# Attention with a sliding window and routed experts: the attention steps put in the order of the array's tiling

## The chip, the cores and the metric

One core of one Trainium2 chip runs the program. The metric is the device time of one execution in microseconds (us). A core has five engines that run their own instruction lists and wait for each other by semaphores: TensorE (PE, with the loads of its stationary operand shown apart as PEld), VectorE (DVE), ScalarE (ACT), GpSimd (POOL) and SyncE (SP, which only issues DMAs here). Each engine works through its list in order.

## The reference

Eight batches of eight heads: 512 local positions and 32 global ones, head size 64. A local query sees the 32 global keys and the local keys within 32 positions; a global query sees all 544 keys. Then every token goes through one of eight experts, chosen by a gate and sticky along the sequence.

```python
s_g = scale * q_g @ k_all.T;  out_g = softmax(s_g) @ v_all
s_ll = where(abs(pos_i - pos_j) <= 32, scale * q_l @ k_l.T, -1e9)
a_l = softmax(concat([scale * q_l @ k_g.T, s_ll]))
out_l = a_l @ concat([v_g, v_l])
x = concat([out_g, out_l])              # per batch: 544 tokens, 512 wide
e = argmax(x @ w_gate)  or the expert before it, by a local gate
out = p[e] * (relu(x @ w1[e]) @ w2[e])
```

## The kernel before

The first third of the program is attention, the rest the experts; the change is in attention alone. The work of a batch is six units: four local ones, `l0` to `l3`, each a pair of heads, and two global ones, `g0` and `g1`, each two pairs. They follow each other as l0 l1 g0 l2 g1 l3, batch after batch, 48 in all, and the loop in `run` makes one step for each of them. In the step of unit number s, the scores and exponentials of unit s are made, and the probabilities of unit s-2 are transposed and multiplied with v. So in the step that is called l1 below, the scores are those of l1 and the v products are those of l3 of the batch before.

What a step is made of, by its functions:

- `l_s` makes one half (`hb` 0 or 1) of a local unit's scores: a matmul writes the mask into a PSUM bank (bf16, all 128 columns of the array), then eight products of 128 rows by 64 columns add q k. `g_s` makes the scores of a global unit, also 64 columns wide.
- `l_max` on DVE takes the row maxima of such a bank and subtracts them; `l_exp` on ACT takes the exponential. The second half's exponential is put off into the step after (`late`). `g_max` and `g_exp` do this for a global unit.
- `l_t` and `g_t` transpose the probabilities on PE (128 by 128) into two banks, and ACT copies each bank to SBUF.
- `l_av` multiplies one half with v: sixteen products, 32 columns wide, into one bank. DVE then adds 1e-9 to the row sums (`rs`), takes their reciprocal and writes the scaled result to `xa`: three instructions, the last of which reads the bank for the last time. `g_av` is the same for a global unit, with `xg`.
- Pieces of the gate's logits are put in between: `f1` transposes 128 columns of a batch's `xa` on PE (four transposes, then a copy by ACT), `f1g` transposes `xg`, `f2` and `f2g` multiply with the gate's weights (32 columns wide), and `f3` transposes the logits back. They wait in the list `fin` and are taken from it in order; a piece can't be taken in the step that put it there. After the v products of a local unit its `f1` is put into the list.

PSUM has eight banks. Scores take four in turn (`ps_s`), transposes two (`ps_t`: `l_t`, `g_t`, `f1`, `f1g`), and the products with v two (`ps_o`: `l_av`, `g_av`, `f2`, `f2g`, and one small product of `f3`). A bank is written again when its last reader is done.

The order of each engine's list is that of the calls in `run`. PE matmuls have three tilings here: 128, 64 and 32 columns of the array. In a local step before, PE's order is: transposes, mask, scores of half 0, perhaps a piece, v product of half 0, mask, scores of half 1, perhaps a piece, v product of half 1.

Of the kernel before, what the change touches and what calls it, by code (L numbers as in the profile page):

```python
# [13 lines left out]
ALU = mybir.AluOpType  # L14
AX = mybir.AxisListType
# [3 lines left out]
P = 128  # L19
# [80 lines left out]
class Attn:  # L100
# [122 lines left out]
    def bank(self, r):  # L223
        return r().rearrange("p (t k) -> p t k", k=P)

    def l_s(self, st, hb):
        nc = self.nc
        if hb == 0:
            b, pr = st["u"]
            if pr == 0:  # L230
                self.cur[b]["xa"] = self.xa()
                self.cur[b]["xg"] = self.xg()
            st["pe"] = self.pe()
        qbd = st["qbd"]
        kf = st["kx"].rearrange("p m c k -> p (m c k)")
        sp = st["sp"] = self.bank(self.ps_s)
        mo = sp.rearrange("p t (k c) -> p t k c", c=32)[:, :, 0::3, :]
        nc.tensor.matmul(mo, self.cst.idb, self.mask[:, 4 * hb:4 * hb + 4], start=True, stop=False, skip_group_check=True)
        for t in range(4):
            for t2 in range(2):  # L240
                w = 8 * hb + 2 * t + t2
                f = 32 * (3 * (w // 2) + w % 2)
                nc.tensor.matmul(sp[64 * t2:64 * t2 + 64, t], qbd[:, w], kf[:, f:f + P], start=False, stop=True, skip_group_check=True)  # L243

    def l_max(self, st, hb):
        nc = self.nc
        mx = self.mx()
        nc.vector.tensor_reduce(out=mx, in_=st["sp"], axis=AX.X, op=ALU.max)  # L248
        self.drip()
        nc.vector.tensor_tensor(out=st["pe"][:, 4 * hb:4 * hb + 4], in0=st["sp"], in1=mx.broadcast_to([P, 4, P]), op=ALU.subtract)  # L250

    def l_exp(self, st, hb):
        pe = st["pe"][:, 4 * hb:4 * hb + 4]
# [166 lines left out]
    def run(self, rt, moe):  # L420
        order = []
        for b in range(B):
            order += [("l", b, 0), ("l", b, 1), ("g", b, 0), ("l", b, 2), ("g", b, 1), ("l", b, 3)]
        units = [{"k": k, "u": (b, i)} for k, b, i in order]
        pairs = [u for u in units if u["k"] == "l"]
        n = len(units)
        fin = []
        when = []

        def fpiece():  # L430
            if fin and when[0] <= s:
                f, a = fin.pop(0)
                when.pop(0)
                if f is not None:
                    f(*a)
# [12 lines left out]
        self.prep(pairs[0])  # L448
        self.blank(1)
        nc.vector.memset(self.pg.t[1], 0.0)  # L450
        npr, late = 0, None
        for s in range(n):
            nx = units[s]
            st = units[s - 2] if s >= 2 else None
            nl = nx["k"] == "l"
            sl = st is not None and st["k"] == "l"
            sg = st is not None and not sl
            if nl:
                if npr + 2 < len(pairs):
# [12 lines left out]
            if sg:  # L472
                self.g_t(st)
            if late is not None:
                self.l_exp(late, 1)
                late = None
            if nl:
                self.l_s(nx, 0)
                self.l_max(nx, 0)
            else:  # L480
                self.g_s(nx)
                self.g_max(nx)
            fpiece()
            if sl:
                self.l_av(st, 0)
            if nl:
                self.l_exp(nx, 0)
                self.l_s(nx, 1)
                self.l_max(nx, 1)
            fpiece()  # L490
            if not nl:
                self.g_exp(nx)
            if sl:
                self.l_av(st, 1)
            if sg:
                self.g_av(st)
            if nl:
                if s in DEFER:
                    late = nx
                else:  # L500
                    self.l_exp(nx, 1)
            if s == 0:
                self.cst.load()
                self.cst.rest()
                self.gens += [self.setup(), rt.setup()]
            if s < 6:
                self.drip(4)
# [12 lines left out]
        self.drip(1000)  # L520
        moe.tail = self.tail(units[n - 2], units[n - 1], fin, rt, moe)

    def tail(self, sg, sl, fin, rt, moe):
        b = B - 1
        fin = [x for x in fin if x[0] is not None]
# [36 lines left out]
        yield from every(rt.kinds(), 3)  # L562
        yield KINDS
        yield from every(rt.rest(self.ps_o), RE)
# [1004 lines left out]
```

## Time and profile before

| What | Value |
|---|---|
| median of 3 runs (lowest, highest) | 706.22 us (705.49, 707.1) |
| the profiled execution | 705.68 us |
| its span, first to last instruction | 704.0 us |
| mean granted clock of TensorE | 0.985 |
| PE, DVE, ACT, POOL busy in the span | 673.2, 428.2, 343.3, 197.7 us |

The profile is of one execution; its span is 1.7 us shorter than its time, and its time 0.5 us below the median. Attention's steps fill the first 230 us or so; the first matmul of the experts starts at 233.75 us. A batch in the middle of attention can be followed by the transposes of `g0` (line 328, in step g1), which start at 102.58 us in one batch and at 130.36 us in the next: 27.78 us for six steps.

### The profile page before, as it was taken

To read this page: it belongs to the slowest core of one execution; us is meant where nothing else is said; L and a number is where in the kernel's file an instruction comes from. 1 tells how busy PE (TensorE), PEld (TensorE's weight loads), DVE (VectorE), ACT (ScalarE), POOL (GpSimd) and SP (SyncE) were. 2 spreads that over 40 slices of the span, in tenths; PEclk is the share of its full clock that TensorE was granted. 3 is DMA by queue.
4 is the path that set the end of the run, shared out by engine and by line. 5 is a ranking of instruction groups with operands and counts; after the bars stand their busy time and mean duration, and the time that the engine had idled before them with its cause. 6 is when DMAs were issued, how large, how long until landed. Compare 5 with 4: busy or idle time off the path is not lost.

```text
span 704.0 us, 18381 instructions
## 1 busy us (share of the span) xinstructions
PE 673.2 (96%) x7253; PEld 564.2 (80%) x7253; DVE 428.2 (61%) x1057; ACT 343.3 (49%) x614; POOL 197.7 (28%) x321
## 2 busy tenths in 40 slices
PE   9999999999899899998998999999999999999991
PEld 7777777777677778887887988889988889899890
DVE  7878777777887787994516625335445325165551
ACT  4565555655355664652325635243535334256551
POOL 7634344243333311132022312040304020223312
PEclk9999999999999999999999999999999999999996
DMA  8966967865756487767319737255557245176561
GB/s 329 383 232 228 354 242 271 324 258 205 292 182 244 173 319 248 269 220 273 131 66 314 241 116 254 70 182 175 195 173 234 98 126 167 65 262 237 187 215 51
DMA packets 43011, 151.44 MB, mean 215 GB/s; under 512 B 7965, under 2 KB 9245, under 8 KB 38688
## 3 DMA queue, kind: packets, MB, share of 16 engines
q1 hardware_dynamic: 35536, 126.92, 50.5%
q0 software_dynamic: 6960, 21.90, 9.3%
q8 instruction: 77, 1.26, 0.7%
q14 instruction: 150, 1.23, 0.6%
q10 hardware_dynamic: 288, 0.13, 0.1%
HBM read 130.55 MB, written 19.69 MB: 213 GB/s over the span
## 4 chain that ended last, share of the span: by engine, by line
PE 59%; DVE 3%; issue 1%; ACT 0%; POOL 0%; DVEq 0%; POOLq 0%; ACTq 0%
PE ps L1262 28%; PE ps L1251 26%; PE ps L1205 3%; DVE wq L1160 1%; DVE wp L1160 0%; PE ps L1374 0%; DVE xT L991 0%; PE ps L999 0%; DVE xl L1160 0%; POOL xa L1191 0%; DVE xT L989 0%; DVE wp L1208 0%; PE ps L276 0%; DVE wq L1366 0%; DVE hh L1160 0%
## 5 line engine op out<-in xcount | busy, mean ns | idle before, releaser
L1268 POOL DMA_INDIRECT out_dram<-y,tk x39 | 40.7, 1042 | 317.9 <-ACT y L1267 297.8
L1262 PE MATMUL ps<-wp,wq 128*128 128x512 f32 x504 | 128.0, 401 | 0.9 <-ACT wq L1365 0.9
L1262 PEld LDWEIGHTS ps<-wp,wq 128*128 128x128 f32 x504 | 93.5, 190 | 20.6 <-ACT wq L1365 1.1
L1251 PE MATMUL ps<-wp,wp 128*128 128x256 f32 (+5 forms) x672 | 109.4, 323 | 0.0
L1251 PEld LDWEIGHTS ps<-wp,wp 128*128 128x128 f32 x672 | 103.8, 189 | 4.8
L1254 DVE SCALAR_TENSOR_TENSOR wq<-ps,wq 128x256 fp32r<-128x256 f32 (+5 forms) x80 | 41.7, 526 | 73.3 <-ACT wq L1253 70.7
L191 POOL TENSOR_SCALAR_AFFINE_SELECT qbd<-raw 64x512 f32<-64x512 f32 x62 | 44.6, 719 | 120.2 <-PE ps L243 100.8
L1208 DVE TENSOR_TENSOR wp<-ps,wp 128x512 fp32r<-128x512 f32 x40 | 27.5, 691 | 79.8 <-ACT wp L1207 79.8
L1253 ACT ACTIVATE wq<-ps 128x256 fp32r<-128x256 f32 (+5 forms) x80 | 37.2, 468 | 78.6 <-PE ps L1251 68.7
L243 PE MATMUL ps<-kx,qbd 128*64 128x128 f32 x1024 | 71.3, 281 | 1.8 <-issue 1.8
L1267 ACT ACTIVATE y<-ps,pp 128x512 f32<-128x512 f32 x39 | 26.9, 690 | 77.3 <-PE ps L1262 71.0
L243 PEld LDWEIGHTS ps<-kx,qbd 128*64 128x64 f32 x1024 | 55.2, 138 | 11.7 <-issue 7.6
L248 DVE TENSOR_REDUCE mx<-ps 128x4 f32<-128x512 f32 x64 | 43.9, 686 | 28.5 <-PE ps L243 28.3
L1160 DVE TENSOR_TENSOR wp<-raw,wp 128x1024 fp32r<-128x1024 f32 x47 | 57.0, 1217 | 2.9 <-ACT wp L1150 2.8
L1191 POOL DMA_INDIRECT xa<-xs,idx x42 | 52.2, 1242 | 17.1 <-issue 10.0
L254 ACT ACTIVATE pe<-pe 128x512 f32<-128x512 f32 x64 | 40.7, 636 | 32.3 <-DVE pe L250 32.3
L1150 ACT CAST wp<-raw 128x1024 fp32r<-128x1024 f32 x49 | 50.8, 1046 | 1.5 <-DMA raw<-in_w_dram 0.7
L1207 ACT CAST wp<-ps 128x512 fp32r<-128x512 f32 x40 | 23.5, 591 | 55.1 <-PE ps L1205 55.1
L250 DVE TENSOR_TENSOR pe<-ps,mx 128x512 f32<-128x512 f32 x64 | 44.1, 688 | 1.6
L276 PE MATMUL ps<-v,pt 128*32 128x65 f32 x2048 | 43.1, 224 | 1.6 <-ACT pe L254 0.6
L276 PEld LDWEIGHTS ps<-v,pt 128*32 128x32 f32 x2048 | 33.7, 111 | 13.1 <-issue 7.5
L191 POOL TENSOR_SCALAR_AFFINE_SELECT kx<-raw 128x384 f32<-128x384 f32 (+3 forms) x127 | 43.1, 372 | 2.9 <-DMA raw<-in_qk_dram 0.8
(279 smaller groups left out, 1172.4 us busy)
## 6 DMA issues: line engine op xcount, KB each, us to landing
raw<-in_w_dram SPq DMA_DIRECT2D x78, 512.0 KB, 3.8
v<-in_vw_dram SPq DMA_DIRECT2D x32, 1040.0 KB, 9.8
raw<-in_qk_dram SPq DMA_DIRECT2D x32, 528.0 KB, 9.4
xa<-in_w_dram SPq DMA_DIRECT2D x26, 512.0 KB, 4.7
xT<-in_w_dram SPq DMA_DIRECT2D x20, 512.0 KB, 4.2
xs<-xa SPq DMA_DIRECT2D x8, 1056.0 KB
qgb<-in_qg_dram SPq DMA_DIRECT2D x8, 128.0 KB
xa<-xs,idx POOLq DMA_INDIRECT x42
```

What stands on the lines that cost most here:

```text
L191: self.nc.gpsimd.affine_select(out=out, in_=in_, pattern=pat, compare_op=ALU.is_ge, fill=0.0, base=0, channel_multiplier=0)
L243: nc.tensor.matmul(sp[64 * t2:64 * t2 + 64, t], qbd[:, w], kf[:, f:f + P], start=False, stop=True, skip_group_check=True)
L248: nc.vector.tensor_reduce(out=mx, in_=st["sp"], axis=AX.X, op=ALU.max)
L250: nc.vector.tensor_tensor(out=st["pe"][:, 4 * hb:4 * hb + 4], in0=st["sp"], in1=mx.broadcast_to([P, 4, P]), op=ALU.subtract)
L254: self.nc.scalar.activation(out=pe, in_=pe, func=AF.Exp, scale=SCALE)
L276: nc.tensor.matmul(o[32 * w4:32 * w4 + 32, g, h], pt[:, 2 * g + w4 // 2, w4 % 2, h, :], v[:, w, h * (D + 1):(h + 1) * (D + 1)], start=True ...
L1150: nc.scalar.copy(out=hi, in_=raw)
L1160: (nc.gpsimd if pool else nc.vector).tensor_tensor(out=lo, in0=raw, in1=hi.bitcast(F32), op=ALU.subtract)
L1191: self.nc.gpsimd.indirect_dma_start(out=self.xr[j] if k == "early" else self.xr4[:, j], out_offset=None, in_=src, in_offset=bass.IndirectO ...
L1251: nc.tensor.matmul(ph, a[:, dc, fs], b_[:, dc, n0:n1], start=(n == 0), stop=(n == 11))
L1254: nc.vector.scalar_tensor_tensor(out=hl[:, fc, n0:n1], in0=ph, scalar=0.0, in1=hh[:, fc, n0:n1].bitcast(F32), op0=ALU.max, op1=ALU.subtract)
L1262: nc.tensor.matmul(py, a[:, fc, js], b_[:, fs], start=(fc == 0 and k == 0), stop=(fc == 7 and k == 2))
```

## The change

The mask's matmuls for both halves get a function of their own, `l_m`, and a step's calls are put into this order: transposes, both masks, pieces that transpose (`f1`, `f1g`, `f3`, up to two), the late exponential, both halves of the scores with their maxima, the exponential of half 0, both halves of the v products, and at the end one piece that multiplies with the gate's weights (`f2` or `f2g`). Each instruction is still issued as often as before.

```diff
+    def l_m(self, st):
...
+        st["sp"] = [self.bank(self.ps_s) for _ in range(2)]
+        for hb in range(2):
+            mo = st["sp"][hb].rearrange("p t (k c) -> p t k c", c=32)[:, :, 0::3, :]
+            nc.tensor.matmul(mo, self.cst.idb, self.mask[:, 4 * hb:4 * hb + 4], start=True, stop=False, skip_group_check=True)
...
-        def fpiece():
-            if fin and when[0] <= s:
+        def fpieces(kinds, most):
+            while most and fin and when[0] <= s and fin[0][0].__name__ in kinds:
...
             if sg:
                 self.g_t(st)
+            if nl:
+                self.l_m(nx)
+            fpieces(("f1", "f1g", "f3"), 2)
             if late is not None:
                 self.l_exp(late, 1)
                 late = None
             if nl:
                 self.l_s(nx, 0)
+                self.l_s(nx, 1)
                 self.l_max(nx, 0)
+                self.l_max(nx, 1)
+                self.l_exp(nx, 0)
             else:
                 self.g_s(nx)
                 self.g_max(nx)
-            fpiece()
+                self.g_exp(nx)
             if sl:
                 self.l_av(st, 0)
-            if nl:
-                self.l_exp(nx, 0)
-                self.l_s(nx, 1)
-                self.l_max(nx, 1)
-            fpiece()
-            if not nl:
-                self.g_exp(nx)
-            if sl:
                 self.l_av(st, 1)
             if sg:
                 self.g_av(st)
+            fpieces(("f2", "f2g"), 1)
...
-                    fin += [(self.f1g, (b,)), (None, ()), (self.f2g, (b,))]
-            if len(fin) > 4:
-                fpiece()
+                    fin += [(self.f1g, (b,)), (self.f2g, (b,))]
```

In the lists below a row is an instruction with its line, what it writes and reads, and its size; `ps_63` to `ps_66` are the banks of the scores, `ps_67` and `ps_68` those of the transposes, `ps_69` and `ps_70` those of the v products. A line of attention has a number that is higher by four after the change (243 is 247, 276 is 280, 352 is 356); the mask is line 238 before and 236 after.

PE in a step l1, before, from the first mask to the transposes of the step after (line 359 is `f1g`):

```order
L238 MATMUL ps_63<-mask,idb 128x4x2x32
L243 MATMUL ps_63<-kx_147,qbd_145 64x128 x8
L359 MATMUL ps_68<-idf,xg_110 128x128
L276 MATMUL ps_70<-v_133,pt_142 32x65 x16
L238 LDWEIGHTS idb
L238 MATMUL ps_64<-mask,idb 128x4x2x32
L243 MATMUL ps_64<-kx_147,qbd_145 64x128 x8
L276 MATMUL ps_69<-v_133,pt_143 32x65 x16
L260 MATMUL ps_67<-idf,pe_137 128x128 x4
L260 MATMUL ps_68<-idf,pe_137 128x128 x4
```

The same place on PE after the change (line 363 is `f1g`, line 379 is `f2g`, line 356 is `f1`):

```order
L236 MATMUL ps_63<-mask,idb 128x4x2x32
L236 LDWEIGHTS idb
L236 MATMUL ps_64<-mask,idb 128x4x2x32
L363 MATMUL ps_68<-idf,xg_110 128x128
L247 MATMUL ps_63<-kx_147,qbd_145 64x128 x8
L247 MATMUL ps_64<-kx_147,qbd_145 64x128 x8
L280 MATMUL ps_70<-v_133,pt_142 32x65 x16
L280 MATMUL ps_69<-v_133,pt_143 32x65 x16
L379 MATMUL ps_70<-xgT_116,wgg 32x32 x4
L264 MATMUL ps_67<-idf,pe_137 128x128 x4
L264 MATMUL ps_68<-idf,pe_137 128x128 x4
L356 MATMUL ps_67<-idf,xa_108 128x128 x4
```

`f1g` has moved ahead of the scores, and `f2g` follows the v products and writes `ps_70`, the bank that the first of them wrote two rows above it; the `f1` of the next step stands ahead of that step's scores.

PE in a step g0, before, from the last scores of g0 on (line 375 is `f2g`, line 352 is `f1`):

```order
L296 MATMUL ps_66<-raw_77,qgb_153 64x288
L296 MATMUL ps_66<-raw_78,qgb_153 64x288
L375 MATMUL ps_70<-xgT_116,wgg 32x32 x4
L276 MATMUL ps_69<-v_134,pt_140 32x65 x16
L352 MATMUL ps_67<-idf,xa_108 128x128 x4
L276 MATMUL ps_70<-v_134,pt_141 32x65 x16
```

The same place on PE after the change (line 300 makes the scores, line 371 is `f2`):

```order
L300 MATMUL ps_66<-raw_77,qgb_153 64x288
L300 MATMUL ps_66<-raw_78,qgb_153 64x288
L280 MATMUL ps_69<-v_134,pt_140 32x65 x16
L280 MATMUL ps_70<-v_134,pt_141 32x65 x16
L371 MATMUL ps_69<-xT,wgl 32x512 x4
```

`f2`, which stood in the step after (step l2), is now at this step's end and writes the bank of the first v product; `f2g` and `f1` have gone to the places shown above.

DVE in a step l1, before (lines 248 and 250 are `l_max`, lines 279, 281 and 284 are the three instructions of `l_av`; lines 771 and 774 are small work of another function):

```order
L248 TENSOR_REDUCE mx_120<-ps_63 128x4
L771 MEMSET xa_109 128x4x7
L250 TENSOR_TENSOR pe_138<-ps_63,mx_120 128x512
L279 TENSOR_SCALAR rs_122<-ps_70 128x4
L774 COPY gx<-tok 32x1
L281 RECIPROCAL rs_122<-rs_122 128x4
L284 TENSOR_TENSOR xa_108<-ps_70,rs_122 128x2x128
L248 TENSOR_REDUCE mx_118<-ps_64 128x4
L250 TENSOR_TENSOR pe_138<-ps_64,mx_118 128x512
L279 TENSOR_SCALAR rs_123<-ps_69 128x4
L281 RECIPROCAL rs_123<-rs_123 128x4
L284 TENSOR_TENSOR xa_108<-ps_69,rs_123 128x2x128
```

The same place on DVE after the change:

```order
L252 TENSOR_REDUCE mx_120<-ps_63 128x4
L254 TENSOR_TENSOR pe_138<-ps_63,mx_120 128x512
L252 TENSOR_REDUCE mx_118<-ps_64 128x4
L254 TENSOR_TENSOR pe_138<-ps_64,mx_118 128x512
L283 TENSOR_SCALAR rs_122<-ps_70 128x4
L285 RECIPROCAL rs_122<-rs_122 128x4
L288 TENSOR_TENSOR xa_108<-ps_70,rs_122 128x2x128
L283 TENSOR_SCALAR rs_123<-ps_69 128x4
L285 RECIPROCAL rs_123<-rs_123 128x4
L288 TENSOR_TENSOR xa_108<-ps_69,rs_123 128x2x128
L381 COPY gsb_114<-ps_70 128x32
```

Both halves of the maxima now stand ahead of everything that reads a v product.

More of the change, by code (lines that the diff above doesn't have):

```diff
@@ L224, in bank @@
         return r().rearrange("p (t k) -> p t k", k=P)
+    def l_m(self, st):
+        nc = self.nc
+        b, pr = st["u"]
+        if pr == 0:
+            self.cur[b]["xa"] = self.xa()
+            self.cur[b]["xg"] = self.xg()
+        st["pe"] = self.pe()
+        st["sp"] = [self.bank(self.ps_s) for _ in range(2)]
+        for hb in range(2):
+            mo = st["sp"][hb].rearrange("p t (k c) -> p t k c", c=32)[:, :, 0::3, :]
+            nc.tensor.matmul(mo, self.cst.idb, self.mask[:, 4 * hb:4 * hb + 4], start=True, stop=False, skip_group_check=True)
     def l_s(self, st, hb):
         nc = self.nc
[L228 to L233, printed above, removed]
         qbd = st["qbd"]
         kf = st["kx"].rearrange("p m c k -> p (m c k)")
-        sp = st["sp"] = self.bank(self.ps_s)
-        mo = sp.rearrange("p t (k c) -> p t k c", c=32)[:, :, 0::3, :]
-        nc.tensor.matmul(mo, self.cst.idb, self.mask[:, 4 * hb:4 * hb + 4], start=True, stop=False, skip_group_check=True)
+        sp = st["sp"][hb]
         for t in range(4):
@@ L247, in l_max @@
         mx = self.mx()
-        nc.vector.tensor_reduce(out=mx, in_=st["sp"], axis=AX.X, op=ALU.max)
+        nc.vector.tensor_reduce(out=mx, in_=st["sp"][hb], axis=AX.X, op=ALU.max)
         self.drip()
-        nc.vector.tensor_tensor(out=st["pe"][:, 4 * hb:4 * hb + 4], in0=st["sp"], in1=mx.broadcast_to([P, 4, P]), op=ALU.subtract)
+        nc.vector.tensor_tensor(out=st["pe"][:, 4 * hb:4 * hb + 4], in0=st["sp"][hb], in1=mx.broadcast_to([P, 4, P]), op=ALU.subtract)
     def l_exp(self, st, hb):
@@ L428, in run @@
         when = []
-        def fpiece():
-            if fin and when[0] <= s:
+        def fpieces(kinds, most):
+            while most and fin and when[0] <= s and fin[0][0].__name__ in kinds:
                 f, a = fin.pop(0)
                 when.pop(0)
-                if f is not None:
-                    f(*a)
+                f(*a)
+                most -= 1
         nc = self.nc
@@ L524, in tail @@
         b = B - 1
-        fin = [x for x in fin if x[0] is not None]
         self.g_t(sg)
```

## The prediction

> **What bounds the kernel now.** I read the page's engine table first, then busy time by stretches of one batch, then PE's instructions in order of time, and last the same for all engines where PE waits for another.
>
> ```profile
> span 704.0 us, 18381 instructions
> PE 673.2 (96%) x7253; PEld 564.2 (80%) x7253; DVE 428.2 (61%) x1057; ACT 343.3 (49%) x614; POOL 197.7 (28%) x321
> L243 PE MATMUL ps<-kx,qbd 128*64 128x128 f32 x1024 | 71.3, 281 | 1.8 <-issue 1.8
> L276 PE MATMUL ps<-v,pt 128*32 128x65 f32 x2048 | 43.1, 224 | 1.6 <-ACT pe L254 0.6
> ```
>
> Busy time by stretches (length, then PE, PEld, DVE, ACT, POOL, the granted clock, DMA): a batch of attention, and a later one that carries more DVE work.
>
> ```profile
> 102.50:130.30 27.80, 27.80 (x596) 21.18 (x587) 21.14 (x73) 16.01 (x37) 11.08 (x25) 1.00 0.77 277
> 158.00:186.00 28.00, 26.49 (x533) 20.40 (x522) 24.13 (x87) 14.89 (x35) 10.40 (x23) 1.00 0.68 247
> ```
>
> PE has no hole in a batch; DVE is busy 76% of it. So today PE's list sets attention's pace, and DVE has 6.7 us of slack a batch. PE's own order over that batch (start, length, instruction):
>
> ```profile
> 102.58 0.88 PE L328 MATMUL ps<-idf,pg 128*128 128x128 f32 x6
> 103.38 1.14 PE L296 MATMUL ps<-raw,qgb 128*64 128x256 f32 x8
> 106.29 1.09 PE L260 MATMUL ps<-idf,pe 128*128 128x128 f32 x8
> 107.22 0.27 PE L238 MATMUL ps<-mask,idb 128*128 128x256 bf16 x1
> 107.42 1.09 PE L243 MATMUL ps<-kx,qbd 128*64 128x128 f32 x16
> 108.45 0.66 PE L276 MATMUL ps<-v,pt 128*32 128x65 f32 x32
> 109.05 0.28 PE L238 MATMUL ps<-mask,idb 128*128 128x256 bf16 x1
> 110.88 0.87 PE L328 MATMUL ps<-idf,pg 128*128 128x128 f32 x6
> 111.59 0.27 PE L238 MATMUL ps<-mask,idb 128*128 128x256 bf16 x1
> 111.79 1.09 PE L243 MATMUL ps<-kx,qbd 128*64 128x128 f32 x16
> 115.51 1.09 PE L260 MATMUL ps<-idf,pe 128*128 128x128 f32 x8
> 116.64 1.09 PE L243 MATMUL ps<-kx,qbd 128*64 128x128 f32 x16
> 117.67 0.33 PE L359 MATMUL ps<-idf,xg 128*128 128x128 f32 x1
> 117.92 0.67 PE L276 MATMUL ps<-v,pt 128*32 128x65 f32 x32
> 120.36 1.09 PE L260 MATMUL ps<-idf,pe 128*128 128x128 f32 x8
> 121.38 1.14 PE L296 MATMUL ps<-raw,qgb 128*64 128x256 f32 x8
> 125.42 1.09 PE L243 MATMUL ps<-kx,qbd 128*64 128x128 f32 x16
> 126.44 1.07 PE L367 MATMUL ps<-xT,wgl 128*32 128x512 f32 x8
> 127.32 0.64 PE L276 MATMUL ps<-v,pt 128*32 128x65 f32 x32
> 130.36 0.88 PE L328 MATMUL ps<-idf,pg 128*128 128x128 f32 x6
> 131.16 1.14 PE L296 MATMUL ps<-raw,qgb 128*64 128x256 f32 x8
> ```
>
> The first scores start at 103.38 (step g1), 107.42 (l3), 111.79 (l0), 116.64 (l1), 121.38 (g0), 125.42 (l2) and 131.16 (g1 again). I follow the change by these starts.
>
> **The change part by part. Fewer changes of tiling.** Sixteen matmuls of a half's scores take 1.09 us from first start to last end, one takes 0.281: (1.09 - 0.28) / 15 = 0.054 from start to start, 0.86 for all. The v product starts 1.03 after them (107.42 to 108.45): 0.17 for going from 64 to 32 columns. In the same way a v product streams for 0.45, and the mask comes 0.60 after its start: 0.15 for 32 to 128. Eight transposes take 0.93 up to a mask (106.29 to 107.22, no change) and 1.02 up to 64-column scores (120.36 to 121.38): 0.09. One transpose (0.12) reaches a v product after 0.25: 0.13. In the order of a batch I count 34 changes before and 20 after: four fewer 128 to 64, four fewer 64 to 128, three fewer each of 32 to 128 and 128 to 32. That is 0.36 + 0.68 + 0.45 + 0.39 = 1.9 us a batch, were PE never made to wait.
>
> **New waits.** In a local step DVE now does both halves' maxima ahead of both halves' v results. What PE needs next from DVE comes later, while PE asks for it earlier. The rows for DVE's pace, all engines in order of time, from two batches:
>
> ```profile
> 113.19 0.20 PEld L352 LDWEIGHTS ps<-idf,xa 128*128 128x128 f32 x2 [0.17 <-DVE xa L284]
> 116.26 1.07 ACT L262 COPY pt<-ps 128x512 f32<-128x512 f32 x2 [1.14 <-PE ps L260]
> 117.78 0.69 DVE L248 TENSOR_REDUCE mx<-ps 128x4 f32<-128x512 f32 x1 [0.79 <-PE ps L243]
> 118.51 0.69 DVE L250 TENSOR_TENSOR pe<-ps,mx 128x512 f32<-128x512 f32 x1
> 131.96 0.88 DVE L304 TENSOR_REDUCE m<-ps 128x1 f32<-128x256 f32 x2
> 132.87 0.21 DVE L306 TENSOR_SCALAR nb<-m 128x1 f32<-128x1 f32 x1
> 134.24 0.16 DVE L342 TENSOR_SCALAR rsg<-ps 128x1 f32<-128x1 f32 x1 [1.16 <-PE ps L339]
> 134.64 0.28 DVE L346 TENSOR_SCALAR xg<-ps,rsg 128x64 f32<-128x64 f32 x1
> 137.68 0.15 DVE L279 TENSOR_SCALAR rs<-ps 128x4 f32<-128x4 f32 x1
> 138.08 0.42 DVE L284 TENSOR_TENSOR xa<-ps,rs 128x256 f32<-128x256 f32 x1
> 138.42 0.68 DVE L248 TENSOR_REDUCE mx<-ps 128x4 f32<-128x512 f32 x1
> ```
>
> The maximum starts 1.14 after its scores (116.64 to 117.78), the subtraction 0.73 later. Four such instructions: the first v result starts 1.14 + 2.90 = 4.04 after the step's first scores. A v result occupies DVE for 0.74 (137.68 to 138.42) and ends 0.82 after its start. So the first ends at +4.86 and the second at +5.60. PE would be through scores and v products at 0.86 x 2 + 0.17 + 0.45 x 2 = +2.8. Now from first scores to first scores, with 0.05 for a semaphore:
>
> - l3 to l0: `f1` transposes what l3's step has just written, ahead of l0's scores. PE is there at about +3.9; the last two of the four transposes wait for +5.60. Then 0.05 + 0.23 + 0.09: 5.97. Before: 4.37, and the same piece, 1 us later in PE's list, waited 0.17 already (113.19). **+1.60**
> - l0 to l1: `f1g` waits for `xg`: 4.04 + 0.68 (134.24 to the end of 134.64's row), + 0.05 + 0.12 + 0.09 = 4.98 against 4.85. **+0.13**
> - l1 to g0: `f2g` stands at +2.8 and writes the bank that the first v result still reads: 4.91. Then 0.1 for its eight small products (8 x 0.014, as in a v product), 0.15, and transposes from 5.16 on. `f1` needs one of their two banks: ACT's copy starts 0.75 after them (115.51 to 116.26) and takes 0.6 (two take 1.07): 6.57. Then 0.47 + 0.09: 7.13 against 4.74. **+2.39**
> - g0 to l2: the global maxima end 0.80 + 1.12 after the scores (131.16, 131.96, 132.87), the first v result 0.82 later, 2.74; `f2` waits for it, from 2.0. `f2` 0.88 (126.44 to 127.32), 0.15, transposes 0.93, masks 0.2, `f3` 0.47 and its small 32-column product 0.05 + 0.13 + 0.15, `f1` 0.47, 0.09: 6.31 against 4.04, in part work moved here from the next interval. **+2.27**
> - l2 to g1: `f1` waits as in the first: 5.97 against 5.74, though `f2` and `f3` left. **+0.23**
> - g1 to l3: less in between: scores 0.91, 0.17, v product 0.67, 0.15, transposes 0.93, masks 0.2, 0.09: 3.12 against 4.04. **-0.92**
>
> Sum: +5.7 us a batch, 27.8 to 33.5. The second mask next to the first is in no row; two masks are between 0.1 and 0.4 together, and 0.2 is nearest to the 0.20 from 107.22 to 107.42, which holds a change of tiling. What is late next: ACT's exponentials are wanted two steps later; score banks have two steps; POOL's copies and the loads get more time. These cost nothing as long as PE and DVE take turns as above.
>
> Seven batches go through all six intervals: +40. The first has only two of the new waits: +1. In the batches from 158 us on DVE has 3 us more to do (24.13 against 21.14); what of it stands in the chain above adds 0 to 4, I take 2.
>
> **The clock.** These stretches are from another place of the same kernel:
>
> ```profile
> 188.00:190.00 2.00, 0.78 (x15) 0.54 (x10) 0.94 (x3) 0.56 (x1) 0.00 (x0) 1.00 1.03 407
> 192.00:194.00 2.00, 2.00 (x38) 1.73 (x30) 1.87 (x11) 0.30 (x1) 1.81 (x5) 0.50 0.09 37
> ```
>
> PE lost 1.2 us of two, and the clock stood at half shortly after. The wait at `f2g` is 2.1 us long. If it drops the clock in three batches, for 1.2 us each, +3.5; the ends are 0, and two slow stretches of up to 1.7 us in each of seven batches, +24. The Trainium skill ("TensorE: Matmul & The Clock Gate", Part 1) puts the drop after an idle window of about 3.4 us; by that no wait here would cost clock, and the sum would end at 749. The trace disagrees, with its drop after a shorter hole.
>
> Sum: 705.7 (the profiled execution; the median is 0.5 higher) + 40 + 1 + 2 + 3.5 = 752.
>
> **The rivals.**
> 1. *Only the changes of tiling count.* Then the waits are hidden and 1.9 us in 7.5 batches come off: 691. It decides at whether DVE's first v result ends by +2.8, where `f2g` stands, and the second by +3.9, where `f1` stands; the rows give 4.86 and 5.60. Against it is also that `f1` waited for `xa` before. The Trainium skill ("TensorEngine Tiling (Array Packing)", Key Properties) says that a change of tiling mode drains TensorE; the rows agree, and this rival is that rule alone.
> 2. *Half of the waits.* If DVE's chain is shorter than the sum of its rows, or PE's moved work fits in DVE's slack in g0 and g1, +3 a batch: 728. For it: DVE has free time in those two steps.
> 3. *The clock falls at nearly every long wait.* Then +24 in place of 3.5: 773. For it: three waits over 1 us in each batch; against: PE is still streaming three quarters of the time.
>
> That the change does something else than grouping can be left out: the order shows 20 changes where 18 would be the least.
>
> **How the numbers follow.** The forecast has 0.72 (its own range 738 to 763: the extra DVE work and mask, and 0 to 12 of clock), rival 1 0.08, rival 2 0.1, rival 3 0.1. The range goes from rival 2's time to rival 3's, 728 to 773, and leaves out rival 1 and some edges. A difference under 0.2% (1.4 us) can't be told from none. Slower 0.91, no change 0.02, faster 0.07.
>
> **What would show it.** In the changed profile a batch (from one step g1's transposes to the next) is 33 to 34 us; PE's idle time, now near nothing, is some 7 us a batch, released by DVE's `xa` and `xg` ahead of lines 356, 363, 371 and 379; DVE's busy time is as before; the experts' part keeps its length. Wrong it would be if lines 379 and 356 start with no wait on DVE, or if DVE makes the v results ahead of the second maximum.

## The result, and the profile after

The changed kernel takes 761.12 us (median of 4 runs, 758.65 to 762.2) against 705.88 us for the kernel before on the same chip (4 runs, 705.49 to 707.1): a ratio of 1.0765, with an interval of 1.0734 to 1.0796. It is 7.6% slower; 752 was forecast, in a range of 728 to 773. The profiled execution took 762.2 us.

From the page of the changed kernel, its span and PE's busy time; then the view by stretches for one batch in the middle and for the two batches that carry the router's work as well (length, then PE, PEld, DVE, ACT, POOL, the granted clock, DMA):

```profile
span 760.3 us, 18403 instructions
PE 680.5 (90%) x7253; PEld 572.1 (75%) x7253; DVE 427.3 (56%) x1057; ACT 346.7 (46%) x614; POOL 197.0 (26%) x321
122.20:155.70 33.50, 27.23 (x590) 21.20 (x587) 21.27 (x73) 16.41 (x38) 10.98 (x25) 1.00 0.65 232
189.30:236.60 47.30, 35.38 (x622) 26.80 (x613) 28.67 (x96) 16.57 (x37) 11.10 (x25) 0.86 0.47 166
236.60:280.70 44.10, 34.11 (x624) 26.31 (x614) 26.14 (x95) 17.43 (x38) 12.35 (x25) 0.85 0.54 198
```

The same two late batches in the kernel before:

```profile
158.20:192.80 34.60, 31.26 (x616) 23.52 (x615) 28.55 (x101) 16.11 (x37) 11.91 (x27) 0.98 0.70 255
192.80:224.30 31.50, 30.16 (x616) 22.97 (x613) 24.97 (x91) 16.23 (x37) 11.89 (x24) 0.97 0.59 226
```

DVE's work is the same (427.3 us against 428.2), PE's matmuls are the same in number; PE now stands idle for 6.3 us in a batch of 33.5. The five batches ahead of the late ones take 34.36, 33.23, 35.14, 33.59 and 33.60 us from one step g1 to the next (before: 27.76 to 27.80), together 31.0 more. The two late ones give 12.7 and 12.5 more; the granted clock in them falls from 0.98 and 0.97 to 0.86 and 0.85. The first matmul of the experts moves from 233.75 to 290.64, by 56.9, and what follows it is as long as before (469.7 us against 470.2).

PE's instructions over the middle batch (start, length, instruction, idle time ahead of it and what ended it), those at the waits and the first scores of each step:

```profile
128.48 1.97 PE L247 MATMUL ps<-kx,qbd 128*64 128x128 f32 x32
...
133.51 0.41 PE L356 MATMUL ps<-idf,xa 128*128 128x128 f32 x2 [0.98 <-DVE rs L283]
134.34 0.44 PE L356 MATMUL ps<-idf,xa 128*128 128x128 f32 x2 [0.42 <-DVE xa L288]
134.71 1.97 PE L247 MATMUL ps<-kx,qbd 128*64 128x128 f32 x32
...
139.49 0.30 PE L363 MATMUL ps<-idf,xg 128*128 128x128 f32 x1 [0.75 <-DVE xg L350]
139.72 1.97 PE L247 MATMUL ps<-kx,qbd 128*64 128x128 f32 x32
141.62 1.12 PE L280 MATMUL ps<-v,pt 128*32 128x65 f32 x64
144.49 0.27 PE L379 MATMUL ps<-xgT,wgg 128*32 128x32 f32 x8 [1.74 <-DVE rs L283]
...
146.07 0.66 PE L356 MATMUL ps<-idf,xa 128*128 128x128 f32 x4 [0.29 <-ACT pt L266]
146.66 1.14 PE L300 MATMUL ps<-raw,qgb 128*64 128x256 f32 x8
149.37 1.07 PE L371 MATMUL ps<-xT,wgl 128*32 128x512 f32 x8 [0.52 <-DVE xa L288]
152.79 1.97 PE L247 MATMUL ps<-kx,qbd 128*64 128x128 f32 x32
157.93 0.41 PE L356 MATMUL ps<-idf,xa 128*128 128x128 f32 x2 [1.31 <-DVE rs L283]
158.95 1.14 PE L300 MATMUL ps<-raw,qgb 128*64 128x256 f32 x8
```

Every wait of the forecast is there, at lines 356, 363, 379 and 371, and but for a short one (0.29 us, for ACT's copy) each is ended by DVE's work on the v products. PE's four largest waits, summed over all of attention (us in total, times, longest):

```profile
PE ps L356 <- DVE rs L283: 18.3, 12, 3.3
PE ps L379 <- DVE rs L283: 9.8, 5, 2.8
PE ps L363 <- DVE xg L350: 5.3, 5, 1.8
PE ps L371 <- DVE xa L288: 4.6, 7, 1.5
```

And DVE in the step l1 above, which shows why: four instructions on the two banks of scores, and only then the v results, the first of which ends at 144.33, 0.16 us ahead of `f2g`.

```profile
140.86 0.69 DVE L252 TENSOR_REDUCE mx<-ps 128x4 f32<-128x512 f32 x1 [1.52 <-PE ps L247]
141.59 0.69 DVE L254 TENSOR_TENSOR pe<-ps,mx 128x512 f32<-128x512 f32 x1
142.19 0.68 DVE L252 TENSOR_REDUCE mx<-ps 128x4 f32<-128x512 f32 x1
142.91 0.69 DVE L254 TENSOR_TENSOR pe<-ps,mx 128x512 f32<-128x512 f32 x1
143.52 0.15 DVE L283 TENSOR_SCALAR rs<-ps 128x4 f32<-128x4 f32 x1
...
143.91 0.42 DVE L288 TENSOR_TENSOR xa<-ps,rs 128x256 f32<-128x256 f32 x1
```

### The profile page after: what moved, and what is told of

Its sections match the earlier page's. It is cut to its first block, busy times and chain, and to the rows that moved or that the text cites. A ratio compares the mean times of both kernels' runs of the same rounds, so it can differ in the third digit from the quotient of the medians.

```text
span 760.3 us, 18403 instructions
## 1 busy us (share of the span) xinstructions
PE 680.5 (90%) x7253; PEld 572.1 (75%) x7253; DVE 427.3 (56%) x1057; ACT 346.7 (46%) x614; POOL 197.0 (26%) x321
## 4 chain that ended last, share of the span: by engine, by line
PE 70%; DVE 22%; issue 3%; ACT 2%; POOL 1%; DVEq 0%; POOLq 0%; ACTq 0%
PE ps L1262 25%; PE ps L1251 23%; PE ps L247 5%; DVE pe L254 4%; DVE mx L252 4%; PE ps L264 3%; PE ps L300 3%; PE ps L356 2%; PE ps L1205 2%; DVE xa L288 2%; PE ps L343 1%; DVE wp L1160 1%; PE ps L371 1%; PE ps L280 1%; DVE wq L1160 1%
## 5 line engine op out<-in xcount | busy, mean ns | idle before, releaser
L1208 DVE TENSOR_TENSOR wp<-ps,wp 128x512 fp32r<-128x512 f32 x40 | 27.4, 690 | 78.5 <-ACT wp L1207 78.5
L247 PE MATMUL ps<-kx,qbd 128*64 128x128 f32 x1024 | 65.1, 280 | 0.6 <-POOL kx L191 0.6
L1160 DVE TENSOR_TENSOR wp<-raw,wp 128x1024 fp32r<-128x1024 f32 x47 | 56.9, 1216 | 2.8 <-ACT wp L1150 2.8
L356 PE MATMUL ps<-idf,xa 128*128 128x128 f32 x128 | 26.3, 314 | 28.7 <-DVE rs L283 18.3
L266 ACT COPY pt<-ps 128x512 f32<-128x512 f32 x64 | 34.8, 594 | 22.0 <-PE ps L264 21.9
L254 DVE TENSOR_TENSOR pe<-ps,mx 128x512 f32<-128x512 f32 x64 | 43.9, 685 | 0.7
```

The source lines that it names most:

```text
L356: nc.tensor.transpose(tp[:, tg], self.cur[b]["xa"][:, tg, P * dc:P * dc + P], self.cst.idf)
L1160: (nc.gpsimd if pool else nc.vector).tensor_tensor(out=lo, in0=raw, in1=hi.bitcast(F32), op=ALU.subtract)
```

## The experiments

The theory: PE loses its time in waits for v results, which DVE makes later while PE's pieces ask for them earlier (or want a bank that they are read from). Rivals: the halved clock; the two maxima side by side on DVE, wherever the pieces stand; grouping as such. The kernel before was timed beside each group of them: 703.02 us (`f2_early`, `f1_late`, `both`, `dve_order`), 702.57 (`f2_bank`, `late_banks`, `fill`, `masks_first`), 706.14 (`f1_mid`, `drip_end`, `mid_drip`) and 701.82 (`mid_f2`). So ratios are compared, not times. A "period" is the time between the transposes of one step g1 and the next.

In `f1_late`, `both` and `mid_f2` a batch's `xa` is written over for the first time ahead of its store, so that part of the stored rows belong to a later batch; the work done is the same.

### Which wait is whose

**f2_early** puts the gate's products ahead of the v products.

```diff
+            fpieces(("f2", "f2g"), 1)
             if sl:
                 self.l_av(st, 0)
                 self.l_av(st, 1)
             if sg:
                 self.g_av(st)
-            fpieces(("f2", "f2g"), 1)
```

> The changed kernel with f2 and f2g put ahead of the two v products instead of behind them; everything else, the 20 changes of tiling a batch included, stays. Theory 'waits' (PE waits for DVE where the order makes it): f2g and f2 no longer wait for the first v result; the interval l1 to g0 becomes 6.0 (6.9 in the changed kernel; f1 in g0 then waits for the second v result instead), g0 to l2 5.4 (6.1), so 31.9 us a batch instead of 33.6, and 744 to 750 us in all. Rival 'tiling' (time goes with the number of changes): 761, no change. Rival 'clock' (the loss is mostly half-speed windows that the long waits cause): the 2 us wait was the longest one, so the half-speed windows in attention go from 10 to about 5 and the time to 750 or less, with the batch without such windows still near 33.6.

Measured: 758.75 us, ratio 1.0791 (1.0746 to 1.0836), so no gain: a miss, and the time that the rival of the tiling alone had. The trace tells the two apart; PE in steps l1 and g0:

```profile
140.07 0.27 PE L379 MATMUL ps<-xgT,wgg 128*32 128x32 f32 x8
140.16 0.64 PE L280 MATMUL ps<-v,pt 128*32 128x65 f32 x32
142.21 0.67 PE L280 MATMUL ps<-v,pt 128*32 128x65 f32 x32 [1.41 <-DVE gsb L381]
...
148.91 0.67 PE L280 MATMUL ps<-v,pt 128*32 128x65 f32 x32 [1.27 <-ACT gsb L372]
```

The wait has moved one instruction on. Two banks serve three writers in such a step, so whoever comes third waits for the reader of the first; the piece's place only decides who that is.

**f2_bank** leaves the order and gives `f2` and `f2g` one of the four banks of the scores.

```diff
-    def f2(self, b):
-        gp = self.ps_o()
+    def f2(self, b, bank=None):
+        gp = (bank or self.ps_o)()
...
-                        fin += [(self.f2, (b,)), (self.f3, (b, rt))]
+                        fin += [(self.f2, (b, self.ps_s)), (self.f3, (b, rt))]
```

(`f2g` likewise.)

> The changed kernel in its own order, but f2 and f2g write one of the four score banks instead of one of the two banks of the v products. Theory 'waits': f2g and f2 now start right behind the v products; l1 to g0 becomes 6.0 (6.9 in the changed kernel; there f1 then waits for the second v result), g0 to l2 5.4 to 5.6 (6.1): 32 to 32.3 us a batch instead of 33.6, 746 to 753 in all. Rival 'tiling': still 20 changes a batch, so 761. That f2_early did not gain is put down to the ring of two: there the second v product waited for the bank that f2 or f2g had taken.

Measured: 743.24 us, ratio 1.0586 (1.0555 to 1.0616). By that ratio it is 747 us beside the 705.88 of before, within the 746 to 753 expected; a batch is a little shorter than expected. Steady periods are 31.35 to 31.71 instead of 33.6. From first scores to first scores l1 to g0 falls from 6.94 to 5.78 and g0 to l2 from 6.13 to 5.41; the other four stay within 0.02. PE's two places now:

```profile
134.15 0.24 PE L379 MATMUL ps<-xgT,wgg 128*32 128x32 f32 x8
...
136.07 0.41 PE L356 MATMUL ps<-idf,xa 128*128 128x128 f32 x2 [0.66 <-DVE rs L283]
```

So 1.9 us of the 5.8 a batch was the bank, not the order. With the wait at `f2g` gone, the next `f1` is the one that waits for DVE.

**dve_order** leaves PE's order and puts DVE's first v result ahead of the second half's maximum.

```diff
                 self.l_max(nx, 0)
-                self.l_max(nx, 1)
                 self.l_exp(nx, 0)
...
             if sl:
                 self.l_av(st, 0)
+            if nl:
+                self.l_max(nx, 1)
+            if sl:
                 self.l_av(st, 1)
```

> The changed kernel's PE order with DVE's order of before: the maxima of half 1 stand behind the first v result again; 20 changes of tiling a batch. Theory 'waits': the first v result ends 3.4 instead of 4.9 us after the step's first scores, the second still at 5.6. So f2g waits 0.7 instead of 2 us, but f1 in the next step still waits for the second: l1 to g0 6.0 instead of 6.9, the other intervals as in the changed kernel; 32.6 us a batch, 750 to 756 in all. Rival 'tiling': 761. Rival 'clock': the longest wait is gone, so 750 or less.

Measured: 753.53 us, ratio 1.0698 (1.066 to 1.0736): the total as expected, but not for the reason given. The wait at `f2g` falls to 0.59 us and l1 to g0 to 5.95; `f1` waits 1.54 for the second v result, which is now later, and the steady period is 34.6. Four of the five steady batches hold a half-speed window, though, in step g1, which takes 4.67 us there and 3.13 elsewhere; without it they would take some 33.0, where 32.6 was expected. The larger gain is in the two late batches (43.9 and 41.8). DVE's order alone doesn't carry the loss; DVE is one chain, and what is put ahead in it delays the rest.

**f1_late** has every piece wait one step more.

```diff
-            when += [s + 1] * (len(fin) - len(when))
+            when += [s + 2] * (len(fin) - len(when))
```

> The changed kernel with each piece of the logits taken one step later than now (f1, f1g, f3, f2 and f2g all shift by a step); 20 changes of tiling a batch. Theory 'waits': f1 no longer waits for the v results of the step just before; f2 (now in step l2) and f2g (now in g0) still wait for the bank of the first v result. A batch is 30 to 31.5 us, 733 to 745 in all. Rival 'tiling': 761. Rival 'clock': no better than 744, because ten half-speed windows cost at most 17 us together.

Measured: 745.34 us, ratio 1.0586 (1.0549 to 1.0624), just above the upper end. The first period, in which `f3` does not stand yet, is 30.94, later ones are 32.8 to 35.9, where 30 to 31.5 was expected: the waits at `f1` are down to 0.66 us (for ACT's copy), but `f2` now waits 2.43 us and the v products up to 2.14, both for DVE's `xa`.

**both** has `f1_late` and `f2_early` together.

> Both edits together: f2 and f2g ahead of the v products, and each piece a step later; 20 changes of tiling a batch. Theory 'waits': PE waits for DVE no more in a batch; what is left is 0.3 to 0.8 us at each f1 for ACT to copy the transposes' bank. 27.8 to 28.5 us a batch (27.8 before the change), 703 to 718 in all. Rival 'tiling': 761. Rival 'clock': no better than 744.

Measured: 727.56 us, ratio 1.0373 (1.0298 to 1.0448): half of the loss is gone, less than expected. Steady periods are 29.6 to 32.6. What is left in one batch, on PE:

```profile
138.94 0.67 PE L280 MATMUL ps<-v,pt 128*32 128x65 f32 x32 [1.58 <-DVE xa L288]
141.40 0.67 PE L280 MATMUL ps<-v,pt 128*32 128x65 f32 x32 [1.79 <-ACT gsb L372]
```

The second is the two banks again; it comes in each of the five steady batches (7.6 us together), the first only in this one.

### The clock

**fill** keeps the order after the change and puts idle transposes, whose result nobody reads, into PE's waits: six ahead of each `f1`, twelve ahead of each `f2g`.

```diff
+            if fin and when[0] <= s and fin[0][0].__name__ == "f1":
+                self.spare(6)
             fpieces(("f1", "f1g", "f3"), 2)
...
+            if fin and when[0] <= s and fin[0][0].__name__ == "f2g":
+                self.spare(12)
             fpieces(("f2", "f2g"), 1)
```

> The changed kernel with idle PE time filled: six transposes of the identity ahead of each f1 and twelve ahead of each f2g, into the bank that is written next anyway; their result is never read. PE's waits for DVE stay, PE is only not idle in them. Theory 'waits': a batch without half-speed windows stays at 33.6 us. The clock: the half-speed windows in attention (10 in the changed kernel, against 1 before) go to 4 or fewer, and the time falls by what they cost, 5 to 12 us, to 749 to 756. If the clock costs nothing beside the waits: 759 to 764.

Measured: 758.95 us, ratio 1.0797 (1.0763 to 1.0831), which can't be told from the change itself. The trace's record of the clock has ten windows of 3.41 us at half speed in attention after the change and three here, and the mean clock over the span goes from 0.966 to 0.983. The third batch after the change, and then the third and the two late ones here:

```profile
87.01:122.15 35.14, 28.88 (x594) 22.19 (x588) 21.34 (x73) 16.61 (x38) 11.07 (x25) 0.95 0.61 219
87.70:121.96 34.26, 31.24 (x624) 24.48 (x618) 21.37 (x73) 16.52 (x38) 11.08 (x25) 1.00 0.63 229
190.75:235.30 44.55, 35.02 (x650) 26.82 (x644) 28.50 (x96) 16.29 (x37) 11.10 (x25) 0.96 0.48 176
235.30:277.45 42.15, 35.38 (x651) 27.94 (x644) 26.51 (x95) 17.14 (x38) 12.29 (x25) 0.92 0.56 207
```

The total hides two effects. The idle transposes are not free: ahead of `f2g` they make l1 to g0 7.59 us instead of 6.94 in a batch without a half-speed window, 0.65 a batch. And the clock has a price: the third batch holds one such window after the change and none here, and with the 0.65 that window cost 1.5 us, by which PE's busy time there also exceeds that of the next batch (28.88 against 27.33 over its 33.60 us). The two late batches lose five of their eight windows and get 4.7 us shorter together (44.55 and 42.15 against 47.31 and 44.10), 6.0 with the fillers' time: 0.9 to 1.2 a window. At 0.9 to 1.5 each, the nine windows that the change adds to the one of the kernel before are some 8 to 14 us of the 55, an estimate. The waits for DVE stay, and with them the larger part of the loss.

### The two late batches

**drip_end** keeps the order too. The router's instructions, which the kernel gives out between DVE's instructions of the maxima and v results, are given out at the end of the step, as many as before.

```diff
     def l_max(self, st, hb):
...
-        self.drip()
+        self.owed.append(False)
...
             fpieces(("f2", "f2g"), 1)
+            self.pay()      # the drips owed, one by one
```

(In `l_av`, `g_max` and `g_av` likewise.)

> The order after the change, but the work of another function (the router's, on DVE, ACT and PE) that is dripped between the instructions of the maxima and of the v results is given out at the end of each step, in the same amounts. Theory (in the two heavy batches this work stands inside DVE's chain of maxima and v results, so that all of it delays the v results that PE waits for): the heavy batches fall from 47.3 and 44.1 us to 38 to 41 each, the steady ones stay at 33.6; total 746 to 752. Rival (the heavy batches are long because the router's own work waits for PE and the other engines, or because of the halved clock): they stay at 45 to 48 and 42 to 45; total 757 to 763.

Measured: 748.24 us, ratio 1.0617 (1.0572 to 1.0663), as the theory had it. The late batches by stretches:

```profile
189.20:228.00 38.80, 29.08 (x621) 23.04 (x613) 30.08 (x96) 16.54 (x38) 11.37 (x25) 1.00 0.55 201
228.00:266.50 38.50, 29.82 (x621) 23.25 (x614) 26.56 (x95) 16.70 (x38) 12.51 (x25) 0.96 0.60 226
```

38.8 and 38.5 us in place of 47.3 and 44.1, with no less DVE work (30.1 and 26.6 us busy); the steady batches take 34.2, with a half-speed window in each but the first. Not all of this is the waits: of the eight half-speed windows in the late batches one is left, and PE is busy 10.6 us less in them (29.1 and 29.8 against 35.4 and 34.1) for as many matmuls. How the work stood in the chain after the change, DVE in a late step l1 (scores from 215.60):

```profile
216.74 0.69 DVE L252 TENSOR_REDUCE mx<-ps 128x4 f32<-128x512 f32 x1 [1.52 <-PE ps L247]
218.62 0.33 DVE L880 TENSOR_TENSOR rv<-ps,oh 128x168 f32<-128x168 f32 x1 [1.19 <-PE ps L873]
...
219.35 0.68 DVE L254 TENSOR_TENSOR pe<-ps,mx 128x512 f32<-128x512 f32 x1
...
222.18 0.56 DVE L905 TENSOR_TENSOR o<-io,plo 128x384 bf16<-128x384 bf16 x1
222.65 0.42 DVE L288 TENSOR_TENSOR xa<-ps,rs 128x256 f32<-128x256 f32 x1
```

The first v result ends 7.5 us after the scores' start, against 4.6 in a steady batch. Some of that is the router's work itself (0.33 at line 880, 0.56 at line 905, others between them), and 1.19 is a wait of that work for PE: its product (line 873) stands behind both halves of the scores, and DVE's in-order list holds the maxima behind it. The granted clock was 0.50 from 216.8 to 220.2 us, which takes in this wait.

### What the grouping gains where nothing waits

**masks_first** is the kernel before with the two masks side by side ahead of the scores, and nothing else moved: 31 changes of tiling a batch in place of 34.

```diff
             if nl:
+                self.l_m(nx)
                 self.l_s(nx, 0)
                 self.l_max(nx, 0)
```

> The kernel before, with one part of the change alone: both masks are written ahead of the first half's scores; pieces, scores, maxima and v products stay as before. 31 changes of tiling a batch instead of 34, and no order that makes PE wait. If a change of tiling costs PE 0.09 to 0.17 us where PE sets the pace: 0.3 to 0.5 us a batch less, 27.3 to 27.5, and 2 to 4 us less than the kernel before in all. If these changes are hidden by other work: no difference.

Measured: 702.13 us (12 runs), ratio 0.9998 (0.9976 to 1.0019): no difference that can be measured; 2 to 4 us were expected. Three of the five steady periods are 27.5 to 27.7 against 27.8, the other two 27.8 and 28.2. The shortest:

```profile
102.80:130.31 27.51, 27.42 (x592) 21.21 (x588) 20.89 (x73) 16.08 (x37) 11.04 (x25) 1.00 0.80 295
```

PE's busy time is 0.2 to 0.4 us below that of the kernel before in each of the five batches (27.4 to 27.6 against 27.6 to 27.8), about 0.1 for each change of tiling; in two of them PE pauses for 0.36 and 0.56 us with no releaser in the profile.

**late_banks** has the pieces one step later (as `f1_late`), all four of them in banks of the scores (as `f2_bank`), and the store of a batch five turns earlier.

```diff
-F4 = 6
+F4 = 1
...
-            when += [s + 1] * (len(fin) - len(when))
+            when += [s + 2] * (len(fin) - len(when))
```

> The changed order with every wait on DVE or ACT taken out that I know: each piece a step later, f1, f1g, f2 and f2g in score banks, and the store of a batch's result five turns earlier, so that xa is stored before it is written again. 20 changes of tiling a batch. Theory 'waits': PE sets the pace again with 14 fewer changes of tiling: 25.9 to 27.3 us a batch (27.8 before the change), 690 to 702 in all, so faster than the kernel before by 0.3 to 2%. Rival: DVE's own chain (4.4 us in a local step) becomes the limit where local steps follow each other: 27.8 or more a batch and no gain.

Measured: 706.61 us (11 runs), ratio 1.0076 (1.005 to 1.0102). Nine tenths of the loss are back, but not the gain expected on top. One of its batches by stretches, to be held against the 27.80 us with 27.80 busy of before; and the one wait of PE over 0.2 us in it:

```profile
99.92:126.96 27.04, 26.18 (x592) 21.32 (x588) 20.30 (x72) 15.71 (x37) 11.06 (x24) 1.00 0.75 287
```

```profile
117.44 0.67 PE L279 MATMUL ps<-v,pt 128*32 128x65 f32 x32 [0.86 <-ACT pe L257]
```

PE is busy 26.2 us (26.4 in the two batches ahead) for as many matmuls as took 27.8 before: fourteen changes of tiling fewer are worth 1.4 to 1.6 us, about 0.1 each (1.9 us in the prediction). Part of it is spent in that batch, more in others: complete periods are 27.0 to 29.0, the late ones 33.0 and 35.1; the first, of 26.2, is without `f3`. In the two longest steady periods, 28.2 and 29.0, PE pauses for 1.45 and 1.35 us with no releaser in the profile. DVE waits for the store of an earlier batch before it may write `xa` again (8.8 us in four waits over all of attention), and POOL, mostly in the late batches, for loads (27.5 in six); what these cost PE is not shown.

**f1_mid** keeps the store where it was and gives no step away. `f1` and `f1g` stand between the scores and the v products of the next step, `f1`, `f1g`, `f2` and `f2g` write banks of the scores.

```diff
-            fpieces(("f1", "f1g", "f3"), 2)
+            fpieces(("f3",), 1)
...
                 self.g_exp(nx)
+            fpieces(("f1", "f1g"), 1)
             if sl:
                 self.l_av(st, 0)
```

> f1 and f1g stand between the scores and the v products of the step after the one that wrote their xa or xg, f2 and f2g stay at the step's end, and all four write banks of the scores; nothing is stored later. 24 changes of tiling a batch, against 34 before and 20 after. Theory (PE's loss is its waits for v results and for banks that they read): the second v result ends 5.6 us after its step's first scores and f1 comes at about +4.4 + 1.9 = 6.3, so it waits no more; f2g and f2 have a bank of their own. A batch then is 27.8 less ten changes at 0.13 us: 26.5, at most 27.5; the two batches with more DVE work 32 to 35 us; total 692 to 703, and faster than before if the batches stay under 27.4. Rival (grouping the two maxima costs by itself, wherever the pieces stand): a batch 29 or more, total 712 or more.

Measured: 713.67 us, ratio 1.0119 (1.0093 to 1.0145). PE's waits for DVE are gone in the steady batches, though DVE still makes both maxima first. So the rival of the two maxima falls, although the total is in its range (712 or more); yet the periods are 28.1 to 29.4, over the 27.5 of the theory. PE in step g0 shows one cause:

```profile
126.07 1.03 PE L371 MATMUL ps<-xT,wgl 128*32 128x512 f32 x6
127.33 1.04 PE L371 MATMUL ps<-xT,wgl 128*32 128x512 f32 x2 [0.23 <-ACT xT L357]
128.31 1.09 PE L264 MATMUL ps<-idf,pe 128*128 128x128 f32 x8
```

`f2` now follows its last `f1` closely, and its last two matmuls wait for ACT's copy. They then take 1.04 us alone, as long as all eight together when none is late (1.07): the products of `f2`, which go to four different column tiles, run side by side, and a late one loses that. `f2` takes 2.24 us in place of 0.88, which is more than the ten changes of tiling bring. Most of the rest is pauses of PE of 0.75 to 0.87 us in three of the five batches for which the profile shows no releaser; what they are is open.

**mid_drip** is `f1_mid` with `drip_end`.

> f1_mid and drip_end together. If the router's work between DVE's instructions is what lengthens the heavy batches, they are 2 to 5 us shorter each than in f1_mid (28 to 31 us), the steady ones the same, and the total is 4 to 8 us below f1_mid's. If DVE's total work sets those batches, no difference to f1_mid within 2 us.

Measured: 721.64 us, ratio 1.0219 (1.0199 to 1.0239): worse than `f1_mid`, where 4 to 8 us less were expected: a miss. The steady batches stay at 28.9; the late ones take 40.8 and 35.2 us against 36.2 and 32.6, and three half-speed windows fall in them, where `f1_mid` has none. Where DVE's results are no longer asked for early, giving the router's work out in one piece is no help; how much of the difference is the clock and which wait costs the most was not separated.

**mid_f2** is `f1_mid` with `f2` one step later.

```diff
-            when += [s + 1] * (len(fin) - len(when))
+            when += [s + 1 + (x[0] == self.f2) for x in fin[len(when):]]
```

> f1_mid with f2 one step later, at the end of step l2, so that f3 and the next f1 follow in step g1. In f1_mid f2 came right behind the copy of its last operand: six of its matmuls went at 126.07, the last two waited until 127.33 and took 1.04 us by themselves (eight together take 1.07), 2.24 us in all where f2 takes 0.88 in the kernel before. Theory (that wait and the lost overlap are what is left of f1_mid's loss): 1.3 us a batch off, steady batches 26.8 to 27.7 against 27.8 before and 28.1 to 29.4 in f1_mid; total 9 to 10 us below f1_mid, a ratio to before of 0.995 to 1.004. Rival (the fewer changes of tiling are worth nothing, whatever waits): batches stay at 28 or more, ratio 1.008 to 1.013.

Measured: 711.55 us, ratio 1.0128 (1.0105 to 1.0151), a miss by the total. The wait that it was made for is gone (g0 to l2 takes 3.95 us against 6.67 in `f1_mid`). In its place, on DVE and then on PE in step l2:

```profile
132.49 0.42 DVE L288 TENSOR_TENSOR xa<-ps,rs 128x256 f32<-128x256 f32 x1 [5.33 <-DMA xs<-xa]
```

```profile
133.06 0.81 PE L280 MATMUL ps<-v,pt 128*32 128x65 f32 x32 [2.89 <-DVE xa L288]
```

`f2` one step later makes the router's logits and with them the store of `xa` later, and the second of only two `xa` buffers is wanted again before that store is through. DVE waits 5.3 us, PE 2.9. The rival of this run (that fewer changes are worth nothing) doesn't follow from its periods (29 to 31.5 after a first of 26.2), since a new wait fills them and the first is without `f3`.

No version here beats the kernel before; `masks_first` is level with it.

## Why the prediction was right

**The path.** Right in kind and place: DVE's v results come later, PE's pieces ask earlier, and the waits stand at lines 356, 363, 379 and 371. `f1_late`, `f2_bank`, `both` and `late_banks` took the waits away one after the other and brought the time from 1.0765 to 1.0076 with the grouping still in place.

**The steady batch.** 33.5 forecast; 33.59, 33.60 and 33.23 measured in the three without a half-speed window. By interval, forecast and measured in the first of these: l3 to l0 5.97 and 6.23, l0 to l1 4.98 and 5.01, l1 to g0 7.13 and 6.94, g0 to l2 6.31 and 6.13, l2 to g1 5.97 and 6.16, g1 to l3 3.12 and 3.13. The misses of up to 0.26 have both signs: the first two transposes of `f1` wait too (0.98 us, for the first v result), where only the last two had been expected to, and DVE's chain to the first v result takes 4.6 us and not 4.86. The mechanism was right at each wait; that the sum is right to 0.1 us is in part luck, since these misses cancel.

**The late batches.** Here lie 8 of the 10 us between the sum and the profiled execution; most of the rest is in the two steady batches with a half-speed window (34.36 and 35.14). The sum had 5.7 us each, 2 for DVE's extra work in both, and 3.5 of clock, some 17; they cost 25.2. Two terms were too small. One is "what of it stands in the chain above adds 0 to 4, I take 2". Its 3 us of extra DVE work were read from a stretch of 28 us, while these batches last 34.6 and 31.5 before the change and hold 7.4 and 3.8 us of DVE work more than the 21.14 of a steady one (28.55 and 24.97). `drip_end`, which takes this work out of the chain, makes them 14 us shorter (77.3 us together against 91.4). With seven half-speed windows fewer, at the 0.9 to 1.5 us that `fill` shows for one, some 7 to 11 of these are the clock, and 3 to 7 are left for the work's place in the chain, where 2 were taken. Whether the clock's part would have come back as waiting was not tested.

**The clock.** This is the other term, and by these estimates the larger one: 3.5 us, in three drops, were forecast, and ten windows at half speed came, nine more than before, for some 8 to 14 us. The price of 1.2 us for a drop was about right, their number was not; eight of the ten stand in the late batches, where the waits are longest. The Trainium skill ("TensorE: Matmul & The Clock Gate", Part 1) puts the drop after a whole idle window of about 3.4 us; here no idle stretch of PE in attention is longer than 3.34 us and the clock still falls, mostly behind windows of 3.41 us in which PE was idle for 1.8 us or more.

**The rivals.** Of rival 2 (half of the waits) nothing is left, since all six intervals came out within 0.26 us. Rival 3's drops of the clock did come, at nearly every long wait of the late batches, but ten windows are fewer than its fourteen stretches, and 0.9 to 1.5 us each is less than its 1.7: the clock's cost lies between the 3.5 of the forecast and its 24 us.

**The gain.** 1.9 us a batch from fewer changes of tiling was somewhat too much: `late_banks` shows 1.4 to 1.6 of PE's busy time for the same fourteen, and `masks_first` 0.2 to 0.4 for three, which its total does not show. It is real, but about a fifth of what the waits cost (5.8 us a batch net, and so 7.2 to 7.4 before this gain). Rival 1, in which only this counts, is refuted by the change itself; the Trainium skill's rule that a change of mode drains the array ("TensorEngine Tiling (Array Packing)", Key Properties) agrees with the 0.1 us each, and says nothing on what the order costs elsewhere.

## What to carry to other kernels

When instructions of a busy in-order engine are regrouped, first follow what each of them needs from the next engine and when that engine, in its own order, can have it; a saving of 0.1 us for each switch is soon lost to one wait of 1.7. Long waits can also bring the clock down, which has a price of its own. A wait that is moved without freeing what it waits for (a bank of a ring of two, a buffer that waits for its store) comes back one instruction, or one step, later. Work that is dripped into another chain's gaps is harmless as long as nobody waits for that chain, and has to be costed, over the whole batch that holds it, as soon as somebody does.

## What was not expected of the hardware

The clock fell in waits shorter than the window: after the change each drop lasts one or two windows of 3.41 us, and windows with 1.8 us or more of idle PE were followed by one (at 1.75 us and less mostly not, once at 1.55). The bound is not sharp in other orders: in `dve_order` a drop followed 1.22 us of idle PE in its window, and in `drip_end` an idle stretch of 3.54 us (from 190.08 us on), split over two windows (counted on from the drops) as 1.83 and 1.71, was followed by none. A product into one of four column tiles takes as long alone as four do together (1.04 against 1.07 us). And PE made pauses with no releaser in the profile, of 0.75 to 0.87 us in `f1_mid` and up to 1.35 in `late_banks`, that one in the middle of 48 like products; the steady batches of the kernel before have none (a late one has one of 1.84). Their cause is open.
